# Grouped-query attention decode on one Trainium2 core: V loads issued by GpSimd instead of SyncE

## The chip, the core and the metric

The kernel runs on one core of a Trainium2 chip. The metric is device time in microseconds (us) of one execution. TensorE is PE in the profile, VectorE is DVE, ScalarE is ACT, GpSimd is POOL, SyncE is SP. All runs quoted are of the state "fast", and each kernel is compared with runs of the kernel before on the same chip. The profiler's span is about 2 us shorter than the timed execution.

## The reference, cut to what matters

```python
B, Hq, Hkv, Sq, Sk, D = 1, 32, 8, 1, 65536, 128        # all bf16

def reference(q, k, v):
    k = jnp.repeat(k, 4, axis=1)                         # 4 query heads share one K/V head
    v = jnp.repeat(v, 4, axis=1)
    scores = jnp.einsum("bhqd,bhkd->bhqk", q, k) * D ** -0.5
    p = softmax(scores, axis=-1)
    return jnp.einsum("bhqk,bhkd->bhqd", p, v)
```

One query token attends to 65,536 cached tokens in 8 groups. K and V are 134 MB each and are read once. There is almost no arithmetic for each byte.

## The kernel before

A group's K is cut into four tiles of 128 partitions x 32 KB (4.19 MB), V likewise: 64 tiles. All of them go through one pool of five buffers, and SyncE issues every load. K runs one group ahead of V, so that the softmax of a group is done when its V arrives: the sequence is K(0,0..3), then K(1,0), V(0,0), K(1,1), V(0,1) and so on.

```python
iopool = ctx.enter_context(tc.tile_pool(name="iopool", bufs=5))
ktp = ctx.enter_context(tc.tile_pool(name="ktp", bufs=4))

def load(view, name, cuts=()):
    t = iopool.tile([P, T * D], bf16, name=name, tag="io")
    edges = [0, *cuts, T]
    for lo, hi in zip(edges, edges[1:]):
        nc.sync.dma_start(out=t[:, lo * D:hi * D], in_=view[:, lo * D:hi * D])     # L72
    return t
# ... q4, ident, sel, one ...
nc.gpsimd.memset(Z[:, :, :, :, :], 0.0)                                            # L106

def k_step(g, j):
    kt = load(k_view[g, j], "kt")
    # ...
    for i in range(NI):                                   # NI = 8
        kT = ktp.tile([P, CW * D], bf16, name="kT")
        nc.vector.transpose(...)                          # L128, DVE, kT <- a part of kt
        for be in range(4):
            nc.tensor.matmul(out=S[:, j, :NCOL], ...)     # L136, PE, scores S

def softmax(g):                                           # after K(g,3)
    nc.vector.reduce_max(out=mx, in_=S, ...)              # L147
    nc.tensor.transpose(out=ps_t, in_=mx, ...)            # L149, PE
    # ... m4 (L151), mrow, nm on DVE; exp on ACT (L167); E = transpose of it on DVE (L172)

def v_step(g, j):
    vt = load(v_view[g, j], "vt")
    # ... 32 matmuls (L200): A += E(g,j) x vt

seq = [("k", 0, j) for j in range(NQ)]
for g in range(Hkv):
    for s in range(NQ):
        if g + 1 < Hkv:
            seq.append(("k", g + 1, s))
        seq.append(("v", g, s))
```

The very last V tile is loaded in five pieces (`CUTS`), so V has 36 load instructions and K has 32. The order of instructions on each engine is set by a compiler's scheduler, not by the program alone.

Of the kernel before, what the change touches and what calls it, by code (L numbers as in the profile page):

```python
# [18 lines left out]
def kernel(  # L19
# [19 lines left out]
    nc = tc.nc  # L39
    P = nc.NUM_PARTITIONS  # L40
    B, Hq, Sq, D = q.shape
# [23 lines left out]
    k_view = k[0].rearrange("g (j p t) d -> g j p (t d)", j=NQ, p=P)  # L65
    v_view = v[0].rearrange("g (j p t) d -> g j p (t d)", j=NQ, p=P)

    def load(view, name, cuts=()):
        t = iopool.tile([P, T * D], bf16, name=name, tag="io")
        edges = [0, *cuts, T]  # L70
        for lo, hi in zip(edges, edges[1:]):
            nc.sync.dma_start(out=t[:, lo * D:hi * D], in_=view[:, lo * D:hi * D])  # L72
        return t

    q4 = const.tile([P, D], bf16)
# [4 lines left out]
    for g in range(Hkv):  # L80
# [9 lines left out]
        out=sel[:, :], in_=ident[:, :].rearrange("p (s c) -> p c s", s=NQ),  # L90
# [4 lines left out]
        out=selh[:, :], in_=sel[:, :].rearrange("p (i h) -> p h i", h=HPG),  # L95
# [11 lines left out]
    for a in range(NQ):  # L107
        r = slice(a * QP, (a + 1) * QP)
        z0 = QP - HPG + a * QP
        for b in range(2):  # L110
            for e in range(2):
                nc.vector.tensor_copy(  # L112
                    out=Z[r, b, e, :, z0:z0 + HPG], in_=qT_v[r, b, e, :, :]
# [5 lines left out]
    A_tiles = {}  # L119

    def k_step(g, j):
        kt = load(k_view[g, j], "kt")
        if j == 0:
            S_tiles[g] = pss.tile([P, NQ, 512], fp32, name="S")
        S = S_tiles[g]
        for i in range(NI):
            kT = ktp.tile([P, CW * D], bf16, name="kT")
            nc.vector.transpose(  # L128
                out=kT[:, :].bitcast(i32),
                in_=kt[:, i * CW * D:(i + 1) * CW * D].bitcast(i32),  # L130
            )
            kT_v = kT[:, :].rearrange("q (c b p e) -> q b e c p", b=2, p=QP, e=2)
            for be in range(4):
                b, e = be // 2, be % 2
                w0 = QP - HPG - i * HPG
                nc.tensor.matmul(  # L136
                    out=S[:, j, :NCOL],
                    lhsT=Z[:, b, e, g, w0:w0 + P],
                    rhs=kT_v[:, b, e, :, :],
                    start=(i == 0 and be == 0),  # L140
                    stop=(i == NI - 1 and be == 3),
                )
# [40 lines left out]
    CUTS = (T // 2, 3 * T // 4, 7 * T // 8, T - T // 16)  # L183
    EDGE = CUTS[-1]

    def v_step(g, j):
        vt = load(v_view[g, j], "vt")
        if j == 0:
            A_tiles[g] = [
                psa.tile([P, HI * D], fp32, name=f"A{u}") for u in range(2)  # L190
            ]
        A = A_tiles[g]
        E = E_tiles[g]
        end = NQ - 1 if g < Hkv - 1 else last_a
        vt_v = vt[:, :].rearrange("p (u i c d) -> p u c i d", u=2, i=HI, c=CW)
        for c0 in range(0, CW, NQ):
            for u in range(2):
                for s in range(NQ):
                    c = c0 + s
                    nc.tensor.matmul(  # L200
                        out=A[u][s * QP:(s + 1) * QP, :],
                        lhsT=E[:, j, c, :],
                        rhs=vt_v[:, u, c, :, :],
                        start=(j == 0 and c0 == 0),
                        stop=(j == end and c0 == CW - NQ),
                    )

    def collect(g, stop):

        A = A_tiles.pop(g)  # L210
        As = [apool.tile([P, HI, D], fp32, name=f"As{u}") for u in range(2)]
        nc.scalar.copy(out=As[0][:, :, :].rearrange("p i d -> p (i d)"), in_=A[0][:, :])
        nc.vector.tensor_copy(out=As[1][:, :, :].rearrange("p i d -> p (i d)"), in_=A[1][:, :])  # L213
        ps_f = psm.tile([HPG, D], fp32, name="ps_f", tag="misc")
        for i in range(NI):
            nc.tensor.matmul(  # L216
                out=ps_f[:, :], lhsT=sel[:, i * HPG:(i + 1) * HPG],
                rhs=As[i // HI][:, i % HI, :],
                start=(i == 0), stop=(stop and i == NI - 1),
            )  # L220
        return ps_f

    def store(g, ps_f, dma):
        o = stats.tile([HPG, D], bf16, name="o")
        nc.vector.tensor_scalar_mul(out=o[:, :], in0=ps_f[:, :], scalar1=rl_tiles.pop(g)[:, :])
        dma.dma_start(out=out[0, g * HPG:(g + 1) * HPG, 0, :], in_=o[:, :])

    def last_step(g, j):


        vt = load(v_view[g, j], "vt", CUTS)
        E = E_tiles.pop(g)
        Dp = psm.tile([P, D], fp32, name="Dp", tag="misc")
        nc.vector.memset(Dp[:, :], 0.0)

        def slot(t, dst, start, stop):
            i, c = t // CW, t % CW
            nc.tensor.matmul(
                out=dst, lhsT=E[:, j, c, i * HPG:(i + 1) * HPG],
                rhs=vt[:, t * D:(t + 1) * D], start=start, stop=stop,  # L240
            )

        ps_f = collect(g, False)
        for t in range(EDGE):
            s = t % NQ
            slot(t, Dp[s * QP:s * QP + HPG, :], t < NQ, t >= EDGE - NQ)
        Ds = stats.tile([P, D], fp32, name="Ds")
        nc.vector.tensor_copy(out=Ds[:, :], in_=Dp[:, :])
        for t in range(EDGE, T):
            slot(t, ps_f[:, :], False, False)  # L250
        nc.tensor.matmul(
            out=ps_f[:, :], lhsT=selh[:, :], rhs=Ds[:, :], start=False, stop=True
        )
        store(g, ps_f, nc.sync)

    for kind, g, s in seq:
        if kind == "k":
            k_step(g, s)
            if s == NQ - 1:
                softmax(g)  # L260
        else:
            if g == Hkv - 1 and s == NQ - 1:
                last_step(g, s)
            else:
                v_step(g, s)
                if s == NQ - 1:
                    store(g, collect(g, True), nc.scalar)
# [30 lines left out]
```

## Time and profile before

| | |
|---|---|
| time, median (range) of 3 runs | 635.18 us (635.05 to 635.27) |
| profiled span | 633.7 us |
| bytes moved by the load queue | 268.44 MB |
| share of the 16 DMA engines' span on that queue | 98.7% |
| DVE busy, PE busy | 54%, 59% |

The page of the kernel before gives first the busy time of each engine (us, share of the span, instructions). The two rows after it show the span in 40 equal slices: tenths of DMA busy time, and GB/s moved.

```profile
PE 376.3 (59%) x2314; PEld 151.0 (24%) x2314; DVE 344.5 (54%) x342; ACT 21.7 (3%) x25; POOL 4.9 (1%) x7
...
DMA  9999999999999999999999999999999999999995
GB/s 366 430 429 429 430 435 434 429 430 435 431 429 432 430 429 430 433 434 431 431 432 427 430 432 430 429 430 434 429 431 429 432 429 430 431 432 432 429 424 232
```

After the first slice the stream stays at 427 to 435 GB/s until the last two, while neither DVE nor PE is near full. The queue table and the table of issues (engine, instructions, KB each, median us from issue to landing) show one queue for all loads:

```profile
q1 hardware_dynamic: 9800, 268.44, 98.7%
...
kt<-in_k_dram SPq DMA_DIRECT2D x32, 4096.0 KB, 46.1
vt<-in_v_dram SPq DMA_DIRECT2D x31, 4096.0 KB, 39.9
```

A tile costs 4.19 MB / 430 GB/s = 9.8 us of stream, but it lands 46.1 or 39.9 us after its issue. So four to five tiles are always under way or queued. This is why SyncE's long waits for a free buffer, in the waits of its queue (waiter, releaser, us in total, times, longest us), cost nothing:

```profile
SPq L72 <- DVE kT L128: 304.1, 32, 15.9
SPq L72 <- DMA kt<-in_k_dram: 160.7, 27, 7.4
```

### The profile page before, as it was taken

The numbers are of one execution on the slowest core, as the hardware profiler recorded it, in microseconds if no ns is written. First come the engines' busy times: TensorE is split into PE (matmuls) and PEld (weight loads), VectorE is DVE, ScalarE is ACT, GpSimd is POOL, SyncE is SP. The second block draws the span as 40 slices with busy tenths as digits, with TensorE's granted clock in tenths as the row PEclk, the third lists the DMA queues.
The fourth block names the chain that finished last, engine by engine and source line by source line (L and its number), as shares of the span: only waits on it lengthen the run. The fifth ranks groups of instructions, "written<-read, shape, count | busy, mean of one in ns | idle before, by whom it ended". The sixth has DMA issues, their size and how long they took to land.

```text
span 633.7 us, 5456 instructions
## 1 busy us (share of the span) xinstructions
PE 376.3 (59%) x2314; PEld 151.0 (24%) x2314; DVE 344.5 (54%) x342; ACT 21.7 (3%) x25; POOL 4.9 (1%) x7
## 2 busy tenths in 40 slices
PE   0696846785457745477544775547664476644825
PEld 0232312231122311133211332113221132211313
DVE  0899834774338753376533765437554375553600
ACT  0000100010000000010000100001000010000100
POOL 3000000000000000000000000000000000000000
PEclk9999888877788967789677986779976799767867
DMA  9999999999999999999999999999999999999995
GB/s 366 430 429 429 430 435 434 429 430 435 431 429 432 430 429 430 433 434 431 431 432 427 430 432 430 429 430 434 429 431 429 432 429 430 431 432 432 429 424 232
DMA packets 10071, 268.82 MB, mean 424 GB/s; under 512 B 1344, under 2 KB 1344, under 8 KB 1728
## 3 DMA queue, kind: packets, MB, share of 16 engines
q1 hardware_dynamic: 9800, 268.44, 98.7%
q8 instruction: 18, 0.29, 0.2%
q10 hardware_dynamic: 248, 0.04, 0.0%
q14 instruction: 5, 0.04, 0.0%
HBM read 268.47 MB, written 0.01 MB: 424 GB/s over the span
## 4 chain that ended last, share of the span: by engine, by line
DMA 70%; PE 12%; DVE 9%; issue 7%; ACT 1%; ACTq 0%; DVEq 0%
DMA kt<-in_k_dram 56%; DMA vt<-in_v_dram 12%; PE S L136 8%; DVE kT L128 8%; DMA q_85<-in_q_dram 2%; DVE mx L147 1%; PE ps_f L216 1%; ACT ET L167 1%; PE A_1900 L200 0%; PE A_772 L200 0%; PE A_773 L200 0%; PE A_1901 L200 0%; DVE Z L112 0%; PE A_396 L200 0%; ACTq L77 0%
## 5 line engine op out<-in xcount | busy, mean ns | idle before, releaser
L136 PE MATMUL S<-kT,Z 128*128 128x512 bf16 x1024 | 283.9, 429 | 207.8 <-DVE kT L128 200.8
L128 DVE STREAM_TRANSPOSE kT<-kt 128x1024 int32<-128x1024 int32 x256 | 292.2, 1207 | 209.0 <-DMA kt<-in_k_dram 208.0
L136 PEld LDWEIGHTS <-Z 128*128 128x128 bf16 x1024 | 108.2, 106 | 381.5 <-issue 300.1
L200 PEld LDWEIGHTS <-E 128*32 128x32 bf16 x992 | 25.1, 100 | 49.4 <-issue 29.6
L167 ACT ACTIVATE ET<-S,nm 128x2048 bf16<-128x2048 f32 x8 | 15.7, 1967 | 575.2 <-DVE nm L164 575.2
L147 DVE TENSOR_REDUCE mx<-S 128x1 f32<-128x2048 f32 x8 | 18.3, 2292 | 10.4 <-PE S L136 10.4
L172 DVE STREAM_TRANSPOSE E<-ET 128x2048 bf16<-128x2048 bf16 x8 | 18.5, 2309 | 3.2 <-ACT ET L167 3.2
L200 PE MATMUL A_2977<-vt,E 128*32 128x512 bf16 x48 | 6.8, 544 | 13.6 <-DMA vt<-in_v_dram 13.6
L213 DVE COPY As_3088<-A_2978 128x512 f32<-128x512 f32 x1 | 0.7, 692 | 22.4 <-PE A_2978 L200 22.4
L149 PE MATMUL ps_t<-ident,mx 128*1 128x128 f32 x8 | 2.3, 283 | 16.9 <-DVE mx L147 16.9
L102 DVE STREAM_TRANSPOSE qT<-q_85 128x64 int32<-128x64 int32 x1 | 0.2, 246 | 16.4 <-DMA q_85<-in_q_dram 16.4
L200 PE MATMUL A_2652<-vt,E 128*32 128x512 bf16 x64 | 8.1, 426 | 0.0
L200 PE MATMUL A_2653<-vt,E 128*32 128x512 bf16 x64 | 7.9, 421 | 0.0
L200 PE MATMUL A_397<-vt,E 128*32 128x512 bf16 x64 | 7.4, 409 | 0.0
L175 PE MATMUL ps_l<-ls,selh 128*4 128x1 f32 x16 | 1.5, 165 | 9.9 <-ACT ET L167 9.9
L200 PE MATMUL A_396<-vt,E 128*32 128x512 bf16 x64 | 7.4, 401 | 0.0
L200 PE MATMUL A_2276<-vt,E 128*32 128x512 bf16 x64 | 7.0, 382 | 0.2 <-DMA vt<-in_v_dram 0.2
L200 PE MATMUL A_1148<-vt,E 128*32 128x512 bf16 x64 | 6.9, 382 | 0.0
L200 PE MATMUL A_1524<-vt,E 128*32 128x512 bf16 x64 | 6.9, 382 | 0.0
L200 PE MATMUL A_1900<-vt,E 128*32 128x512 bf16 x64 | 6.9, 382 | 0.0
L200 PE MATMUL A_772<-vt,E 128*32 128x512 bf16 x64 | 6.9, 382 | 0.0
L200 PE MATMUL A_2978<-vt,E 128*32 128x512 bf16 x48 | 6.9, 548 | 0.0
(95 smaller groups left out, 106.1 us busy)
## 6 DMA issues: line engine op xcount, KB each, us to landing
kt<-in_k_dram SPq DMA_DIRECT2D x32, 4096.0 KB, 46.1
vt<-in_v_dram SPq DMA_DIRECT2D x31, 4096.0 KB, 39.9
vt<-in_v_dram SPq DMA_DIRECT2D x1, 2048.0 KB
vt<-in_v_dram SPq DMA_DIRECT2D x1, 1024.0 KB
vt<-in_v_dram SPq DMA_DIRECT2D x1, 512.0 KB
vt<-in_v_dram SPq DMA_DIRECT2D x2, 256.0 KB
out_dram<-o ACTq DMA_DIRECT2D x7, 1.0 KB
q_85<-in_q_dram ACTq DMA_DIRECT2D x4, 8.0 KB, 6.5
```

The costliest lines, as they stand in the source:

```text
L102: nc.vector.transpose(out=qT[:, :].bitcast(i32), in_=q4[:, :].bitcast(i32))
L128: nc.vector.transpose(out=kT[:, :].bitcast(i32), in_=kt[:, i * CW * D:(i + 1) * CW * D].bitcast(i32),)
L136: nc.tensor.matmul(out=S[:, j, :NCOL], lhsT=Z[:, b, e, g, w0:w0 + P], rhs=kT_v[:, b, e, :, :], start=(i == 0 and be == 0), stop=(i == NI - ...
L147: nc.vector.reduce_max(out=mx[:, :], in_=S[:, :, :NCOL], axis=AX.XY)
L149: nc.tensor.transpose(out=ps_t[:, :], in_=mx[:, :], identity=ident[:, :])
L167: nc.scalar.activation(out=ET[:, :].rearrange("p (a n) -> p a n", a=NQ), in_=S[:, :, :NCOL], func=ACT.Exp, bias=nm[:, :], scale=SCALE, acc ...
L172: nc.vector.transpose(out=E[:, :, :, :].rearrange("p a c r -> p (a c r)"), in_=ET[:, :])
L175: nc.tensor.matmul(out=ps_l[:, :], lhsT=selh[:, :], rhs=ls[:, :], start=True, stop=True)
L200: nc.tensor.matmul(out=A[u][s * QP:(s + 1) * QP, :], lhsT=E[:, j, c, :], rhs=vt_v[:, u, c, :, :], start=(j == 0 and c0 == 0), stop=(j == e ...
L213: nc.vector.tensor_copy(out=As[1][:, :, :].rearrange("p i d -> p (i d)"), in_=A[1][:, :])
L216: nc.tensor.matmul(out=ps_f[:, :], lhsT=sel[:, i * HPG:(i + 1) * HPG], rhs=As[i // HI][:, i % HI, :], start=(i == 0), stop=(stop and i == ...
```

## The change

The intent is to take half of the loads off SyncE's queue: V loads are issued by GpSimd. K loads stay with SyncE. GpSimd's queue is of kind software_dynamic; SyncE's is hardware_dynamic. The text below calls a queue a *ring*, and what is queued there *software* or *hardware descriptors*, after its kind.

```diff
-    def load(view, name, cuts=()):
+    def load(dma, view, name, cuts=()):
         t = iopool.tile([P, T * D], bf16, name=name, tag="io")
         edges = [0, *cuts, T]
         for lo, hi in zip(edges, edges[1:]):
-            nc.sync.dma_start(out=t[:, lo * D:hi * D], in_=view[:, lo * D:hi * D])
+            dma.dma_start(out=t[:, lo * D:hi * D], in_=view[:, lo * D:hi * D])
         return t
@@ k_step
-        kt = load(k_view[g, j], "kt")
+        kt = load(nc.sync, k_view[g, j], "kt")
@@ v_step
-        vt = load(v_view[g, j], "vt")
+        vt = load(nc.gpsimd, v_view[g, j], "vt")
@@ last_step
-        vt = load(v_view[g, j], "vt", CUTS)
+        vt = load(nc.gpsimd, v_view[g, j], "vt", CUTS)
```

The diff does not show a second effect: the scheduler reorders PE. Before, all 32 score matmuls of K(g+1,j) come first, then V(g,j)'s. After the change, for two of the four tiles of nearly every group, V's matmuls are mixed in between K's from the twelfth on. PE keeps to that order, so a V matmul that waits for its tile then also holds up the K matmuls behind it (the waits after show this: 123.8 us). A third difference is in the softmax: on DVE, an accumulator copy (L213) comes earlier among its steps.

## The prediction

> **What bounds the kernel now.** DMA bandwidth. The queue table gives SyncE's queue 98.7% of the 16 engines' span and 268.44 MB; after the first slice the stream stays at 427 to 435 GB/s until the last two. No engine is near it: DVE 54%, PE 59% busy. K and V are 64 tiles of 4 MB: one tile costs 9.8 us of stream (4.19 MB at 430 GB/s), a K/V pair 19.5 us. Compute for a pair is less: eight transposes of K at 1.207 us (9.7 us of DVE), 32 score matmuls (8.9 us), a V step of about 3.5 us. The queue's own waits show SyncE waiting to issue mostly for DVE's transposes, which free a buffer (304 us), yet a load lands 46.1 us (K) or 39.9 us (V) after its issue: four to five tiles are always queued, so these waits hide behind data in flight.
>
> **What the change does.** Same bytes, same five buffers in the same rotation. 36 issues move from SyncE (0.33 us each) to GpSimd, which has 4.9 us of other work. I expect 1 to 2 us each (estimate; the Trainium skill, "DMA: Bandwidth & Descriptors", section "Latency and other measured facts", puts the first byte at about 1 us for software descriptors); behind three queued tiles that is off the critical path. The same page, section "Issuing engines are not separate DMA queues", says all loads still run on the same 16 engines and interleave; this trace has one load queue and can't show it. So the 98.7% resource is not relieved.
>
> The order of landing changes. Before, tiles land one after another. With two rings served in turn, K(n) and V(n) share the bandwidth and land together, every 19.5 us. The pair is then consumed in about 14 us, while three tiles (29 us of stream) are outstanding and each freed buffer is refilled. Even with softmax at a group boundary (about 8 us: maximum 2.3, exponential 2.0, transpose 2.3, small steps) neither ring should run dry. K lands up to 10 us later, but 40 us of V follow the last K. The compiler's order also changes: V matmuls now sit between K's score matmuls on PE, and an accumulator copy comes before softmax steps on DVE. Both lie in slack.
>
> Terms: stream 0; sharing of rings between -4 us (one ring covers the other's gaps between transfers: 434 for 430 GB/s) and +6 us (software descriptors, switching); tail +0.5 us.
>
> **Prediction: 636 us, 8 in 10 between 630 and 647. Faster by over 2%: 2%; within 2%: 86%; slower by over 2%: 12%.**
>
> **In the profile, if right.** A second load queue, of software kind, with 134 MB, K's with 134 MB, shares summing to 97 to 99%; middle slices at 425 to 435 GB/s; some 144 packets per V tile (rows of 32 KB stay whole). Issue to landing about 44 us for K, 29 us for V (estimate: V is issued 10 us after a pair's landing, when its K is transposed, and lands two pairs later). The chain of waits still mostly DMA; DVE and PE busy times unchanged.
>
> **What would make it wrong.** (1) Software descriptors cut rows into small pieces, or the rings disturb each other: middle slices at 400 to 420 GB/s with the share still 98%; 650 to 680 us. (2) One ring takes most of the bandwidth, V fills the buffers while K starves: DMA slices below 9 tenths, DVE waiting for K. (3) DVE holds GpSimd up in writing descriptors: V issues of many microseconds, holes in the DMA row.

## The result and the profile after

The changed kernel takes 635.71 us (median of 6 runs, 635.30 to 635.89), the kernel before in all 635.43 us (6 runs, 635.05 to 635.85). The ratio is 1.0003, with a 95% interval of 0.999 to 1.0016: the same time. Ratios here are the mean time of one kernel's fast runs over that of the other's of the same rounds, so they are not quite the ratio of the medians quoted.

The page after:

```profile
PE 396.7 (63%) x2314; PEld 149.7 (24%) x2314; DVE 346.4 (55%) x342; ACT 22.4 (4%) x25; POOL 24.0 (4%) x43
...
DMA  8999999999999999999999999999999999999995
GB/s 368 441 431 431 432 432 429 432 431 433 427 433 429 430 430 429 435 429 432 429 429 429 430 432 429 434 432 430 430 430 431 432 431 431 429 429 430 427 425 234
```

```profile
q0 software_dynamic: 5056, 134.22, 49.4%
q1 hardware_dynamic: 4616, 134.22, 49.3%
...
kt<-in_k_dram SPq DMA_DIRECT2D x32, 4096.0 KB, 33.8
vt<-in_v_dram POOLq DMA_DIRECT2D x31, 4096.0 KB, 34.8
```

The work is split, 49.4% and 49.3%, and the sum is the old 98.7%. The stream is as full as before (425 to 435 GB/s from the third slice to the last but one, 441 in the second). But loads now land sooner after their issue, 33.8 and 34.8 us for 46.1 and 39.9. With the same bytes in the same time, a shorter time under way means that fewer tiles are queued. By issue count: one K and one V tile pass every 19.5 us, so (46.1 + 39.9) / 19.5 = 4.4 tiles were under way on average before, and (33.8 + 34.8) / 19.5 = 3.5 are now.

The groups of the changed kernel (line, engine, operation, count | busy us, mean ns | idle before, releaser) show what a GpSimd issue costs, 533 ns, and where GpSimd waits:

```profile
L72 POOL DMA_DIRECT2D vt<-in_v_dram x36 | 19.1, 533 | 572.5 <-DVE kT L128 562.7
```

The waits show one that was almost absent before (0.9 us, once): DVE's transposes of K wait for PE, which stands at V's matmuls.

```profile
DVE kT L128 <- PE S L136: 123.8, 33, 9.4
DVE kT L128 <- DMA kt<-in_k_dram: 72.2, 11, 10.3
```

So the profile moved a good deal while the time did not.

**Two counts made from the trace's packet records.** First, who is served: for each stretch of 10 us, each queue's packets give its bytes. In the middle (270 to 350 us of the span) the software queue moves 211 to 217 GB/s and the hardware queue 211 to 218; in the rest of the steady state the halves sway between about 180 and 250. The median packet takes 1.215 us in both, and all data packets but those of the last, cut V tile are whole rows of 32,768 bytes. So the two rings share the bandwidth about evenly, and each tile takes about twice as long: from its first packet to its last 10.9 us in the median before, 20.5 us after (between 100 and 560 us of the span, 128 rows a tile, in order of issue). Second, the *backlog*: 4 MB tiles issued, less the tiles' worth of bytes that the packet records show as moved, taken just before each new issue, between 100 and 560 us of the span. At zero the DMA engines have nothing to do. These are my counts, not a view of the profile. Before: at least 2.77 tiles, median 3.02. After: at least 1.11, median 1.91. The reserve in front of the DMA engines has shrunk from 27 us (2.77 x 9.75 us) to 11 us, and it is still not zero.

### The profile page after: what moved, and what is told of

It is laid out like the page before. It is cut to its first block, busy times and chain, and to the rows that moved or that the text cites. A ratio compares the mean times of both kernels' runs of the same rounds, so it can differ in the third digit from the quotient of the medians.

```text
span 633.4 us, 5482 instructions
## 1 busy us (share of the span) xinstructions
PE 396.7 (63%) x2314; PEld 149.7 (24%) x2314; DVE 346.4 (55%) x342; ACT 22.4 (4%) x25; POOL 24.0 (4%) x43
## 3 DMA queue, kind: packets, MB, share of 16 engines
q0 software_dynamic: 5056, 134.22, 49.4%
q1 hardware_dynamic: 4616, 134.22, 49.3%
## 4 chain that ended last, share of the span: by engine, by line
DMA 62%; PE 17%; DVE 13%; issue 7%; POOL 0%; ACT 0%; SPq 0%; DVEq 0%; ACTq 0%
DMA vt<-in_v_dram 49%; DMA kt<-in_k_dram 13%; PE S L136 10%; DVE kT L128 10%; PE ps_f L216 3%; DVE mx L147 2%; PE A_1900 L200 0%; POOL vt L72 0%; PE A_2652 L200 0%; PE A_1901 L200 0%; ACT ET L167 0%; PE A_2276 L200 0%; PE A_396 L200 0%; PE A_1524 L200 0%; PE A_772 L200 0%
## 5 line engine op out<-in xcount | busy, mean ns | idle before, releaser
L128 DVE STREAM_TRANSPOSE kT<-kt 128x1024 int32<-128x1024 int32 x256 | 297.7, 1214 | 196.9 <-PE S L136 123.8
L136 PEld LDWEIGHTS <-Z 128*128 128x128 bf16 x1024 | 99.0, 104 | 220.0 <-issue 140.6
L200 PEld LDWEIGHTS <-E 128*32 128x32 bf16 x992 | 29.3, 101 | 187.8 <-issue 175.6
L72 POOL DMA_DIRECT2D vt<-in_v_dram x36 | 19.1, 533 | 572.5 <-DVE kT L128 562.7
L200 PE MATMUL A_1900<-vt,E 128*32 128x512 bf16 x64 | 9.9, 474 | 18.8 <-DMA vt<-in_v_dram 18.8
L200 PE MATMUL A_772<-vt,E 128*32 128x512 bf16 x64 | 8.8, 411 | 19.9 <-DMA vt<-in_v_dram 19.9
L200 PE MATMUL A_1148<-vt,E 128*32 128x512 bf16 x64 | 8.8, 412 | 19.0 <-DMA vt<-in_v_dram 19.0
L200 PE MATMUL A_2276<-vt,E 128*32 128x512 bf16 x64 | 9.0, 415 | 17.7 <-DMA vt<-in_v_dram 17.7
L200 PE MATMUL A_1524<-vt,E 128*32 128x512 bf16 x64 | 9.0, 414 | 17.6 <-DMA vt<-in_v_dram 17.6
L200 PE MATMUL A_396<-vt,E 128*32 128x512 bf16 x64 | 9.7, 458 | 15.5 <-DMA vt<-in_v_dram 15.5
L162 PE MATMUL ps_b<-one,mrow 1*128 1x1 f32 x16 | 4.0, 320 | 19.8 <-DVE mrow L156 19.8
L200 PE MATMUL A_2652<-vt,E 128*32 128x512 bf16 x64 | 8.5, 401 | 9.6 <-DMA vt<-in_v_dram 9.6
L200 PE MATMUL A_2977<-vt,E 128*32 128x512 bf16 x48 | 6.7, 486 | 8.3 <-DMA vt<-in_v_dram 8.3
L149 PE MATMUL ps_t<-ident,mx 128*1 128x128 f32 x8 | 2.3, 284 | 12.3 <-DVE mx L147 12.3
L200 PE MATMUL A_1901<-vt,E 128*32 128x512 bf16 x64 | 9.4, 454 | 0.0
L200 PE MATMUL A_397<-vt,E 128*32 128x512 bf16 x64 | 9.3, 447 | 0.0
## 6 DMA issues: line engine op xcount, KB each, us to landing
kt<-in_k_dram SPq DMA_DIRECT2D x32, 4096.0 KB, 33.8
vt<-in_v_dram POOLq DMA_DIRECT2D x31, 4096.0 KB, 34.8
q_85<-in_q_dram ACTq DMA_DIRECT2D x4, 8.0 KB, 14.7
```

What stands on the lines that cost most here:

```text
L72: dma.dma_start(out=t[:, lo * D:hi * D], in_=view[:, lo * D:hi * D])
L128: nc.vector.transpose(out=kT[:, :].bitcast(i32), in_=kt[:, i * CW * D:(i + 1) * CW * D].bitcast(i32),)
L136: nc.tensor.matmul(out=S[:, j, :NCOL], lhsT=Z[:, b, e, g, w0:w0 + P], rhs=kT_v[:, b, e, :, :], start=(i == 0 and be == 0), stop=(i == NI - ...
L149: nc.tensor.transpose(out=ps_t[:, :], in_=mx[:, :], identity=ident[:, :])
L162: nc.tensor.matmul(out=ps_b[:, :], lhsT=mrow[:, :], rhs=one[:, :], start=True, stop=True)
L200: nc.tensor.matmul(out=A[u][s * QP:(s + 1) * QP, :], lhsT=E[:, j, c, :], rhs=vt_v[:, u, c, :, :], start=(j == 0 and c0 == 0), stop=(j == e ...
```

## The experiments

The theory: the kernel is bound by an unbroken stream of bytes over 16 DMA engines; who issues a load, and on how many rings, cannot matter as long as the backlog is not empty. The first rival: two real effects cancelled, a cost of software descriptors and a gain from two rings. Then there is a second question: what made the backlog shrink, the sharing of bandwidth by two rings or the new order on PE, and what would that cost where there is less reserve? Eleven runs were made, and all gave correct results. Every experiment is an edit to the kernel before or to the changed one.

### 1. All loads from GpSimd

```diff
-        kt = load(nc.sync, k_view[g, j], "kt")
+        kt = load(nc.gpsimd, k_view[g, j], "kt")
```

> Both K and V loads from GpSimd: software descriptors only, one ring, and PE and DVE keep exactly the order of the kernel before. Theory (an unbroken stream; who issues does not matter): 635 to 637 us, within 0.4% of before; middle slices 429 to 435 GB/s; the load backlog back to that of before (K about 46, V about 40 us from issue to landing). Rival (two effects cancelled in the change: software descriptors cost something, two rings gain as much): here the cost stands alone, so over 0.5% slower, middle slices below 428 GB/s.

Measured: 640.52 us (5 runs, 640.22 to 640.90), ratio 1.0075 (1.0062 to 1.0088). By its time the rival was favoured. But the slices say otherwise:

```profile
GB/s 236 445 431 430 427 426 433 438 431 430 433 426 427 439 428 429 436 429 430 427 435 426 433 438 429 428 435 429 428 435 430 433 430 433 426 429 435 432 420 219
```

Only the first slice is lower (236 GB/s for 366). From the third slice to the 37th the mean is 430.9 GB/s, and 430.9 in the kernel before; seven of these 35 slices are below the rival's 428, at 426 or 427 (one in the row of before, at 427). The time line of GpSimd in this run (start, us, what) shows why, with SyncE's first issues of the kernel before below it:

```profile
0.88 4.26 POOL L106 MEMSET Z<- 128x4992 bf16 x1
...
5.42 2.76 POOL L72 DMA_DIRECT2D kt<-in_k_dram  x5
```

```profile
0.74 6.81 SPq L72 DMA_DIRECT2D kt<-in_k_dram  x5
```

The first K load stands behind a memset of 4.26 us on GpSimd and is issued 5.42 - 0.74 = 4.7 us later. The span is 638.9 - 633.7 = 5.2 us longer. That had to be tested alone.

### 2. All loads from GpSimd, the memset of Z elsewhere

```diff
-    nc.gpsimd.memset(Z[:, :, :, :, :], 0.0)
+    nc.vector.memset(Z[:, :, :, :, :], 0.0)          # on top of experiment 1
```

> All loads from GpSimd, as in the first experiment, but the 4.3 us memset of Z goes to VectorE, so it no longer stands before the first K load on GpSimd. If the 0.75% of that run was the late first issue (5.4 us after the span's start, 0.7 before), this takes 635 to 636.5 us and the first slice moves 350 GB/s or more again. If software descriptors are slower in the stream, it stays over 638 us.

Measured: 636.64 us (5 runs, 636.12 to 637.26), ratio 1.0019 (1.0007 to 1.0032). The median is 0.14 us above the range that I gave, the first slice is at 359 GB/s, and the rest of the row at 421 GB/s or more up to the last slice. So most of the 0.75% was the late start. What is left is 0.19%, some 1.2 us; the first load still goes out 0.54 us later than from SyncE (at 1.28 us). I did not take the remainder apart further. One ring of software descriptors carries the whole stream at the same rate: the cost in the stream that the rival needs is not there. With one ring the backlog is again at least 2.58 tiles (median 2.85), and the landing times are 44.8 us for K and 39.0 us for V.

### 3. V loads from ScalarE: two hardware rings

```diff
-        vt = load(nc.gpsimd, v_view[g, j], "vt")
+        vt = load(nc.scalar, v_view[g, j], "vt")         # the same in last_step
```

> V loads from ScalarE: two rings, both with hardware descriptors. ScalarE also has the exponentials, so some of its work stands behind a V load that waits for a buffer. Theory: 634 to 640 us, middle slices 429 to 435 GB/s, each queue about 49% of the span; a loss beyond 1% only if holes show in the DMA row because of ScalarE's waits. Rival (two rings gain, hidden by the cost of software descriptors): faster by 0.5% or more, middle slices above 434 GB/s.

Measured: 639.17 us (4 runs, 638.17 to 639.59), ratio 1.0052 (1.0037 to 1.0068). There is no gain from two rings to be hidden. The row of GB/s is full but for the 38th slice:

```profile
GB/s 364 438 443 427 432 430 427 427 430 429 436 433 431 438 427 428 430 427 432 427 432 440 430 429 432 429 428 430 433 429 437 426 434 434 427 430 430 365 426 202
```

In that slice (589 to 605 us) ScalarE has the last loads in its queue, behind the last group's exponential and a store that waits for its data:

```profile
597.40 1.97 ACT L167 ACTIVATE ET<-S,nm 128x2048 bf16<-128x2048 f32 x1 [61.84 <-DVE nm L164]
597.62 0.33 ACTq L72 DMA_DIRECT2D vt<-in_v_dram  x1
...
603.87 0.29 ACTq L226 DMA_DIRECT2D out_dram<-o  x1
604.20 2.88 ACTq L72 DMA_DIRECT2D vt<-in_v_dram  x6
```

The last six load instructions leave from 604.20 us on, right after the store. The slice lost (430 - 365) x 15.9 / 430 = 2.4 us of the 3.3 us by which this span is longer. Most of the loss is that of an issuing engine that does other work, not that of a ring. In the changed kernel GpSimd has no other work after 5.5 us of the span. So both halves of the first rival fall: no gain, and hardly a cost.

### 4. V's loads issued four microseconds late

A memset of the fresh buffer stands before each V load and needs the buffer free, so it delays the issue itself. Two pins keep each memset in front of its load; with them the scheduler left V's matmuls almost unmixed and put the softmax's transpose in front of V(g,3)'s matmuls (its short transpose on PE, L149, follows 1 of the 32 matmuls of V(g,3) in the kernel before, and all 32 in the changed kernel), so the order on PE is nearer to that of before.

```diff
         t = iopool.tile([P, T * D], bf16, name=name, tag="io")
+        if dma is nc.gpsimd:
+            tc.keep_in_program_order(nc.gpsimd.memset(t[:, :4992], 0.0))
...
-            dma.dma_start(out=t[:, lo * D:hi * D], in_=view[:, lo * D:hi * D])
+            tc.keep_in_program_order(dma.dma_start(out=t[:, lo * D:hi * D], in_=view[:, lo * D:hi * D]))
```

> The change, with a memset of the fresh V buffer (4.3 us on GpSimd, about eight times the 0.53 us of an issue) between the buffer coming free and V's load, 31 times, 132 us in all. Theory (an issue is hidden as long as the backlog, at least 1.1 tiles or 10.8 us in steady state, outlasts it): 635 to 638 us. Rival (time at the issue shows up in the span): 31 times 4.3 us, up to 760 us; a partial exposure at group ends only would be 8 times 4.3 us, 670 us.

Measured: 635.50 us (4 runs, 635.26 to 635.82), ratio 0.9996 (0.9983 to 1.0010). The instructions of the V tile on GpSimd (count, min/median/max ns, first and last start):

```profile
L72 POOL DMA_DIRECT2D vt<-in_v_dram x36: 527/527/673, 33.4 to 602.0; - x36
L69 POOL MEMSET vt<- x32: 4252/4257/4277, 28.8 to 595.3; 128x4992 bf16 x32
```

GpSimd is busy for 160.3 us in place of 24.0. The 136 us more stand between a free buffer and a load, and none of it shows in the time. With five buffers an issue is hidden, even one that takes nine times as long (4.26 + 0.53 us).

### 5. The change with V's matmuls after K's, as before

A scheduling edge from each V matmul to the last K matmul of the step before puts PE back to "all of K, then V". It does not put back the rest of the old order: the softmax's transpose still follows all 32 matmuls of V(g,3), and DVE keeps the changed kernel's order (an accumulator copy earlier among the softmax steps).

```diff
-                nc.tensor.matmul(out=S[:, j, :NCOL], ...)
+                last_k[0] = nc.tensor.matmul(out=S[:, j, :NCOL], ...)
@@ v_step
-                    nc.tensor.matmul(out=A[u][...], ...)
+                    after_k(nc.tensor.matmul(out=A[u][...], ...))   # order only, no semaphore
```

> The change, with V's matmuls of a step held behind all of K's score matmuls of the step before, as the kernel before has them. All views agree on the time: 635 to 637 us. What it tells apart is why fewer loads are queued after the change (by my count of bytes issued less bytes moved, at least 1.1 tiles of 4 MB just before an issue in steady state, 2.8 before the change). If the sharing of the bandwidth by two rings does it, the least backlog stays at 1.0 to 1.6 and the issue-to-landing times at 33 to 36 us. If the compiler's interleaving of V between K's matmuls does it, the backlog goes back to 2.3 to 2.8 and the two times add up to 80 us or more.

Measured: 635.69 us (4 runs, 635.57 to 635.88), ratio 0.9999 (0.9986 to 1.0013). The landing times:

```profile
kt<-in_k_dram SPq DMA_DIRECT2D x32, 4096.0 KB, 41.0
vt<-in_v_dram POOLq DMA_DIRECT2D x31, 4096.0 KB, 43.9
```

They add up to 84.9 us, close to the 86.0 of before, but the backlog is only half way back: at least 1.95 tiles (2.77 before, 1.11 after), median 2.62. Neither expectation was met. The mixing of V's matmuls among K's takes about 0.84 tile (1.95 - 1.11). The other 0.82 (2.77 - 1.95) lies in what this edit leaves changed: the two rings, the place of the softmax's steps on PE, and DVE's order. Two things point to the rings, but do not isolate them. Each tile still takes 20.4 us from its first packet to its last, so one more tile is half moved while it holds a whole buffer. And in experiment 4, where the softmax's transpose is not held up (it starts 0.06 us after the maximum ends; here 4.1 to 5.5 us in the middle groups), the same count gives at least 1.5 tiles, with issues that come 4.26 us (0.44 tile) late.

### 6 to 9. Less reserve: four and three buffers

The time cannot show a reserve that is not used up. So buffers were taken away, in the kernel before and in the changed one.

```diff
-    iopool = ctx.enter_context(tc.tile_pool(name="iopool", bufs=5))
+    iopool = ctx.enter_context(tc.tile_pool(name="iopool", bufs=4))      # and 3
```

> The kernel before with four load buffers for five. Theory (a backlog of loads keeps the stream unbroken; before has at least 2.8 tiles queued just before a steady-state issue, so one buffer less leaves 1.8): 635 to 639 us, middle slices still at 427 GB/s or more. If the five buffers were already needed, over 1% slower.

> The change with four load buffers. At five its least backlog is 1.1 tiles, so four leave 0.1: the stream should just begin to break at group ends: 636 to 650 us, and slower than before with four buffers. If the change spent no slack that matters, it equals before with four buffers within 0.3%.

> The kernel before with three load buffers. Backlog by the same count at least 0.8 tiles: 636 to 655 us; holes in the DMA row, if any, once for each group of four K tiles, at softmax.

> The change with three load buffers. By the same count 0.9 tiles short at the worst place of each of 8 groups, some 9 us each: 680 to 760 us, DMA slices below 9 tenths, and clearly slower than before with three buffers (by 4% or more). If the change spent no slack, it equals before with three buffers within 0.5%.

Measured (4 runs each, all against the same 7 runs of the kernel before, median 635.47 us):

| buffers | before: us (ratio) | changed: us (ratio) | before: least backlog | changed: least backlog |
|---|---|---|---|---|
| 5 | 635.47 | 635.71 (other runs) | 2.77 tiles | 1.11 tiles |
| 4 | 635.40 (0.9999) | 635.67 (1.0002) | 1.64 | 0.35 |
| 3 | 637.64 (1.0034) | 647.03 (1.0182) | 0.65 | 0.01 |

With three buffers the change costs 1.0182 / 1.0034 - 1 = 1.5%. (The interval of 1.0182 is 1.0156 to 1.0209: slower for certain, but whether by 2% is unclear.) The scheduler ordered this kernel anew: only 2 to 5 of the 32 matmuls of one V tile in four are mixed in, and the softmax's transpose follows 21 to 32 of V(g,3)'s. The rows of GB/s, first of before and then of the changed kernel, both with three buffers:

```profile
GB/s 367 441 431 432 344 428 429 436 435 432 433 430 435 429 428 429 428 431 430 431 429 432 437 434 431 430 431 431 428 427 428 433 430 433 428 435 435 432 428 242
```

```profile
GB/s 381 431 419 429 332 440 421 444 429 410 431 428 438 425 370 433 438 423 439 374 447 424 431 438 346 438 423 439 432 385 428 424 443 426 390 424 449 422 423 237
```

Before has one dip, in the first group (344 in the fifth slice). That dip is before 100 us and so outside the stretch in which the backlog was counted. The changed kernel dips in every group: 332, 410, 370, 374, 346, 385, 390. The slices are 16 us long and a group takes about 80, so the dips are five slices apart. I had the direction right for both kernels and the size wrong for the changed one: I expected 680 to 760 us and it took 647. Subtracting two whole tiles from the backlog ignored, as I read it, that the loop corrects itself: when one ring is empty, the other has all of the bandwidth (432 GB/s by the packet records of this run, at 137 to 140 us for one), and its tile lands sooner. With four buffers I also expected the stream "just to begin to break" at 636 us or more; it took 635.67 us, and the 0.35 tile that is left is enough.

The waits say what the groups' ends have in common (waiter, releaser, us in total, times, longest us), before and changed, three buffers:

```profile
PE A L200 <- DMA vt<-in_v_dram: 17.3, 4, 7.7
DVE m L151 <- PE ps_t L149: 2.7, 7, 0.5
```

```profile
PE A L200 <- DMA vt<-in_v_dram: 92.2, 21, 9.3
DVE m L151 <- PE ps_t L149: 13.1, 4, 6.2
```

V's matmuls wait 92.2 us for their tile, not 17.3, and the softmax step after the maximum waits 13.1 us, not 2.7. One group's end in the changed kernel's time line with three buffers (start, us, what, and in brackets the idle time before it and its releaser):

```profile
285.26 2.29 DVE L147 TENSOR_REDUCE mx<-S 128x1 f32<-128x2048 f32 x1 [1.27 <-PE S L136]
...
290.23 3.15 PE L200 MATMUL A<-vt,E 128*32 128x512 bf16 x25 [5.00 <-DMA vt<-in_v_dram]
293.30 0.08 PEld L149 LDWEIGHTS ps_t<-ident,mx 128*1 128x1 f32 x1 [0.84 <-issue]
...
304.54 0.14 PEld L136 LDWEIGHTS <-Z 128*128 128x128 bf16 x2 [0.43 <-issue]
...
310.93 0.53 POOL L72 DMA_DIRECT2D vt<-in_v_dram  x1 [26.12 <-DVE kT L128]
```

The maximum of the scores starts at 285.26 us. The next step of the softmax, a short transpose on PE (ps_t), has its place among V's matmuls, and these wait until 290.23 us for their tile. So it comes at 293.30, the scores of the next group start only at 304.54, and the buffer of their K tile is free for a V load only at 310.93. Meanwhile the rings run dry: from 308 to 312 us the windows show 283 GB/s. Sharing makes the V tile later: from its first packet to its last a tile takes 13.1 to 20.1 us in this kernel and 10.8 to 11.0 us in the kernel before with three buffers. But the place of the softmax's steps adds to the delay. Experiments 10 and 11 were made to tell what costs.

### 10. One software ring with three buffers

Experiment 2 with `bufs=3`. PE's order is exactly that of before.

> The same with three buffers: one ring of software descriptors, PE order as before, little backlog. If the loss of the change at three buffers (647.0 against 637.6 us) comes of two rings or of the order, not of software descriptors, this equals before with three buffers: 636.5 to 639.5 us. If GpSimd's issues (0.53 us and their latency) are what is exposed, it is near 647.

Measured: 636.37 us (4 runs, 636.07 to 637.94), ratio 1.0019 (1.0005 to 1.0033). That is not slower than the kernel before with three buffers (1.0034 in its rounds), though every issue is GpSimd's. Its least backlog is 0.63 tiles. Software descriptors are not what costs.

### 11. Two rings with three buffers, V's matmuls after K's

Experiment 5 with `bufs=3`. The trace shows that this changes little: with three buffers hardly any of V's matmuls were mixed in to begin with, and the softmax's transpose and DVE's steps stand exactly where they stand in experiment 9.

> The change with three buffers and the PE order of before (V's matmuls after all of K's). If the sharing of bandwidth by two rings costs the backlog, most of the loss stays: 643 to 650 us. If the compiler's interleaving costs it, 636 to 640 us.

Measured: 646.99 us (4 runs, 645.17 to 648.83), ratio 1.0191 (1.0172 to 1.0210). The rest of the mixing gone, the loss stays. (The profiled execution of this kernel is the fastest of its four, with a span of 643.3 us.) Its row still has the dips, once a group:

```profile
GB/s 371 444 424 423 330 429 444 428 425 396 442 432 425 428 390 428 440 431 430 413 428 427 438 433 387 435 432 428 429 414 425 437 428 435 372 441 440 423 425 266
```

Experiments 10 and 11 settle that GpSimd and its descriptors do not cost the 1.5% (10), nor the mixing of V between K's matmuls (11). I took them to leave only the two rings, but the traces do not allow that. Experiments 8 and 10 have one ring and the old place of the softmax's steps; 9 and 11 have two rings and the new one. One group's end, first with one ring (experiment 8), then in experiment 11:

```profile
281.12 2.29 DVE L147 TENSOR_REDUCE mx<-S 128x1 f32<-128x2048 f32 x1 [1.73 <-PE S L136]
283.47 0.27 PE L149 MATMUL ps_t<-ident,mx 128*1 128x128 f32 x1 [2.06 <-DVE mx L147]
287.19 2.31 DVE L172 STREAM_TRANSPOSE E<-ET 128x2048 bf16<-128x2048 bf16 x1 [0.45 <-ACT ET L167]
```

```profile
286.06 2.29 DVE L147 TENSOR_REDUCE mx<-S 128x1 f32<-128x2048 f32 x1 [1.12 <-PE S L136]
291.27 3.04 PE L200 MATMUL A<-vt,E 128*32 128x512 bf16 x25 [5.25 <-DMA vt<-in_v_dram]
294.24 0.27 PE L149 MATMUL ps_t<-ident,mx 128*1 128x128 f32 x1
299.60 2.30 DVE L172 STREAM_TRANSPOSE E<-ET 128x2048 bf16<-128x2048 bf16 x1
```

At the six group ends between the first and the last, the softmax takes 8.4 to 9.8 us from the start of its maximum to the end of its last transpose in experiments 8 and 10, and 14.7 to 16.3 us in 11. Of this, PE's wait for the V tile in front of ps_t is 3.5 to 6.1 us in 11. The two rings can explain that part: in the old order, too, one V matmul stands before ps_t and would wait. The rest goes with the new order: 20 to 31 more V matmuls in front, an earlier accumulator copy, and transposes of K between DVE's softmax steps. How much of the 1.5% is the rings' and how much the order's is not shown. Two rings with the whole order of before, at three buffers, would tell; that run was not made.

No experiment pointed to a version that beats the kernel before by a margin that counts. The bytes alone take 268.44 MB / 430 GB/s = 624 us of the 633.7 us span.

## Why the prediction was right

The time was right, 636 us for 635.71, and so was its reason: a saturated stream that the change does not relieve. Point by point:

- *"So the 98.7% resource is not relieved."* Right: 49.4% + 49.3% afterwards. The Trainium skill, "DMA: Bandwidth & Descriptors", section "Issuing engines are not separate DMA queues", says that all loads run on the same 16 engines; the trace agrees.
- *"Two rings served in turn, K(n) and V(n) share the bandwidth."* Right: 211 to 217 and 211 to 218 GB/s side by side. The same page, section "Queues, rings and completion order", has the engine switch between rings at the end of a packet; the packet records, rows of 32 KB and 1.215 us in the median on both queues, do not contradict it. Only the halves were seen, not the switching itself.
- *"I expect 1 to 2 us each"* for an issue on GpSimd: too much. It took 0.53 us (0.68 at most). It was off the critical path as said, and experiment 4 shows that 4.8 us would have been too, with five buffers.
- *"Sharing of rings between -4 us and +6 us."* Both ends are empty. No gain: from the third slice to the 37th the mean is 430.6 GB/s with the change and 430.9 before. Software descriptors: at most the 1.2 us of experiment 2, about half of it in the first issue.
- *"Three tiles (29 us of stream) are outstanding."* Mis-sized. The least backlog is 1.11 tiles or 11 us, the median before an issue 1.91 tiles. The mechanism held only because five buffers were more than needed. The prediction spoke of slack and did not say how much of it the change used up.
- *"Both lie in slack"*, of the new order on PE: right for the time (experiment 5: the same), but not free: its mixing takes 0.84 tile of backlog, and DVE waits 123.8 us for PE, 0.9 us before.
- *Issue to landing "44 us for K, 29 us for V"*: measured 33.8 and 34.8. As I read it, the estimate took a K tile's buffer to come free at once after its pair, while in the trace K's transposes wait for PE at V's matmuls. The sum, 73 for 68.6, was nearer than its parts.
- *"DVE and PE busy times unchanged"*: DVE yes (346.4 for 344.5 us), PE no (396.7 for 376.3 us). PE's busy time also moved between the variants of equal time (403.8 in experiment 5, 377.3 in experiment 4). Why is open; its granted clock was 0.805 in this run for 0.829 before. It had no effect on the time.
- Of the three ways to be wrong, none came about. The third was GpSimd held up by DVE. The Trainium skill, "SBUF — State Buffer", section "SBUF: two separate sides", has a warning on it: DVE operations of certain kinds can keep GpSimd from writing descriptors. Here the 36 issues took 527 to 676 ns beside 346 us of DVE work, so nothing of it shows; DVE's work here is mostly 32-bit transposes, and no run tried another kind.

## What to carry to other kernels

If the DMA row is at its ceiling in every slice, do not expect a second issuing engine or ring to give anything (here none did): look at how many loads are queued before you look at who issues them. Two rings share the bandwidth, so tiles that used to land one by one land in pairs, each holding its buffer for longer (20.5 us under way for 10.9). Moving a load also let the compiler reorder other engines. Both are invisible while buffers are plentiful; together they cost 1.5% at three. An experiment that is to put an order back has to be checked in its trace, all of the engine's steps: experiment 11 put back less than it seemed. Equal time is not an equal kernel: compare issue-to-landing times, and take a buffer away from both, to see what a change has spent. If an engine is to issue loads, see what stands before the first and the last of them in its queue: those two places, and not the stream, cost most of the 0.75% and the 0.5% of experiments 1 and 3.

## What the Trainium skill lacked or had wrong

- "DMA: Bandwidth & Descriptors", section "Where 436 GB/s comes from", says that about 358 GB/s on the HBM side binds a load from HBM. Here the loads run at 427 to 435 GB/s, with the program on one core alone, which is at the page's other figure, 435, for the fabric. (The page's own table has 425 GB/s for a 16 MB load on one core; the sentence does not make that exception.)
- The same page, "Rules for kernel authors", says that spreading loads over issuing engines does not help. It lacks what it does to a tile: with two rings each takes 20.5 us from its first packet to its last, for 10.9 us, and holds its buffer for that time. It also lacks that the change can hurt: with the compiler's new order the backlog went from 2.77 tiles to 1.11 and, at three buffers, the time up by 1.5%; the rings' own share is not isolated.
- The same page gives about 1 us to the first byte on the software path and calls the making of descriptors small and variable, with no duration of an issue. The GpSimd issue of a 4 MB load took 0.53 us here, and SyncE's 0.33 us.
- The same page has as "typical" packets of some 9 to 17 descriptors. In the changed kernel 8,064 of the 9,672 packet records of both queues are single rows of 32 KB, and 1,092 have 4 bytes. Whether one record is one packet in the page's sense is not shown.
- No page has that the scheduler's order of matmuls changes when a load moves to another issuing engine. The mixing of V's matmuls among K's took 0.84 tile of backlog here, and the order changed again with the number of buffers.
